# A gated sum of attention and a token mixer: w2 through the buffers of w1, and the last 64 features in both row halves

## The chip, the cores and the metric

The kernel runs on one core of a Trainium2 chip. A time is device microseconds (us) from the launch to the end on that core. The profile is one further execution, recorded instruction by instruction; its span runs from the first instruction to the last.

The engines are TensorE (PE; its weight loads are listed apart as PEld), VectorE (DVE), ScalarE (ACT), GpSimd (POOL) and SyncE (SP), which here issues all transfers.

## The reference

All is float32, with S = 2048 tokens, D = 640 channels, 32 heads of 20 channels and F = 1728 features:

```python
g = sigmoid((x * gate_w).sum(-1, keepdims=True))
a = attention(x, wq, wk, wv) @ wo           # 32 query heads share one key and one value head
h = layernorm(x)                            # (S, D)
u = gelu(einsum("sd,sf->df", h, w1) + b1)   # (D, F): the mixer works along the tokens
b = (einsum("df,fs->ds", u, w2) + b2).T     # (S, D)
out = g * a + (1 - g) * b
```

F is 13 x 128 + 64. The features are worked in 14 chunks of 128, the last of which has only 64 (`FC` = 14, `FT` = 64).

## The kernel before

**Products in three parts.** For precision each float32 operand is split into a high part, its rounding to the matmul type float32r, and a low part, the remainder. A product of two matrices is the sum of three: high by high, high by low, low by high. A block of weights is read raw from memory, and then POOL makes the high part with a copy (line 113 for w1, line 662 for w2) and the low part with a subtraction (lines 114 and 663).

**Row halves.** The 128 rows of TensorE are used as two halves of 64. A matmul with 64 rows or fewer in one half can run beside one in the other. Where both halves add into the same PSUM bank, the kernel lets only one of them do so at a time: a one-element memset on VectorE (`flag`, line 602) marks the last product of one half, and the first of the other half waits for it.

**The main loop** has 488 phases, one for each step of the attention: 32 blocks of four heads by 512 queries (`n`), each with 16 key blocks (`kb`). A phase holds

- four score matmuls for the exponentials (line 589, 62 rows), each followed by an exponential on ACT (line 592);
- four score matmuls that find the row maxima for a later block (line 419, 60 rows), each followed by a maximum on VectorE (line 422), through three PSUM banks;
- a share of the mixer's products, or of the attention's output projection, as filler (`fs`): all of it in one row half, the halves alternating from phase to phase;
- last, four matmuls of the probabilities by the values (line 616, 32 columns each, all 128 rows), which the profile shows as eight passes.

The function `beside` writes TensorE's order for a phase. One lane, in one row half, has the four scores and three of the maximum's matmuls. The other lane, in the other half, has the products, then the flag, then the tile's eviction if the tile ends here, then the fourth maximum's matmul. `beside` merges the lanes by fixed costs (0.232 and 0.147 per matmul).

**The filler.** `batches` cuts each tile's products into entries; an entry is two phases, one per row half, and gives each phase its share of that half's products. The list `seq` of entries is fixed in length, 244, and holds in this order:

- 18 tiles of w1 products (line 843: a chunk of 128 features by 320 channels, 16 token blocks, 48 products in each half), five entries each. The first ten tiles are done before the main loop;
- two empty entries, between which the first columns of w2 are read and split;
- 16 tiles of w2 products (line 682: 128 tokens by 320 channels, for both halves of the channels), four entries for each half tile. A half tile has 81 products: three for each half of the 13 full chunks, and three for the last chunk, in the lower half alone, so 42 and 39;
- eight tiles of the attention's output projection (line 791), 15 products in each half for each half tile. A half tile gets two entries as long as there are some to spare (`twice`), and then one.

What is left over goes into the last 24 steps of the attention, behind the main loop (line 748).

A half tile of products is summed in one PSUM bank, of which there is one (`ps_g`). `done` evicts it: for w2, ACT scales it and adds the bias (line 690), and a half tile later SP stores the row block to scratch memory.

**The weights.** w1 comes in blocks of 512 token rows by 128 features (`w1_load`, `w1_upto`), through three raw buffers (`w1r`) and four pairs of split ones (`w1p`), on the right side of the memory. A block is split as soon as the products of the block four before it are issued, and raw blocks are fetched two ahead. In the last chunk the 64 missing columns are set to zero (line 109). Behind the last w1 entry `second` closes these pools and opens two others: one raw buffer of seven chunks by 128 columns of w2 (`w2r`), and three pairs of split ones (`w2p`). Two of them hold the 14 chunks of one tile. `load` splits, `raw` fetches; both are hung on the entries of the tile before. The rows that the tail needs later (`spare_row`) take buffers of `w2p`.

On every engine the instructions run in the order in which the program lists them; within a phase the list is: TensorE's lanes, evictions, the postponed steps of the attention's normalisation (`settle`: a reciprocal on VectorE, line 628; a multiply on POOL, line 629; a transpose on VectorE, line 632; two splits on POOL), the loads hung on the entry (`rest`), and the values' matmuls.

Of the kernel before, what the change touches and what calls it, by code (L numbers as in the profile page):

```python
# [9 lines left out]
F32 = mybir.dt.float32  # L10
F32R = mybir.dt.float32r
# [6 lines left out]
P = 128  # L18
S, D, H, DH, F = 2048, 640, 32, 20, 1728
NS = S // P  # L20
DC = D // P
FC = (F + P - 1) // P
FT = F - (FC - 1) * P
HD2 = D // 2
# [13 lines left out]
def mix_kernel(ctx: ExitStack, tc: tile.TileContext, A_x, A_wq, A_wk, A_wv, A_wo,  # L38
               B_x, B_w1, B_b1, B_w2, B_b2, gate_w, out):
    nc = tc.nc  # L40
# [3 lines left out]
    def f32(ap):  # L44
        return ap.bitcast(F32)
# [30 lines left out]
    right = ExitStack()  # L76
    ctx.callback(right.close)
    w1r = right.enter_context(tc.tile_pool(name="w1r", bufs=3, side="right"))
    w1p = right.enter_context(tc.tile_pool(name="w1p", bufs=4, side="right"))

    HS = NS // 4
    chunks = [(d, fc, hf) for d in range(2) for fc in range(FC) for hf in range(4)]
    w1t = {}
    fetched = [0]

    w1raw = {}

    def w1_load(n):
        while len(w1raw) < min(n, len(chunks)):
            c = len(w1raw)  # L90
            d, fc, hf = chunks[c]
            fw = P if fc < FC - 1 else FT
            wr = w1r.tile([P, HS, P], F32, name="wr")
            nc.sync.dma_start(
                out=wr[:, :, :fw],
                in_=B_w1[hf * HS * P:(hf + 1) * HS * P, fc * P:fc * P + fw].rearrange("(c p) f -> p c f", p=P))
            w1raw[c] = wr

    def w1_upto(n):
        while fetched[0] < min(n, len(chunks)):  # L100
            c = fetched[0]
            w1_load(c + 1)
            d, fc, hf = chunks[c]
            fw = P if fc < FC - 1 else FT
            wr = w1raw[c]
            wh = w1p.tile([P, HS, P], F32R, name="wh")
            wl = w1p.tile([P, HS, P], F32R, name="wl")
            if fw < P:
                nc.gpsimd.memset(wr[:, :, fw:], 0.0)
            if c < 4 * PRO:  # L110
                nc.scalar.activation(wh, wr, AF.Copy)  # L111
            else:
                nc.gpsimd.tensor_copy(wh, wr)
            nc.gpsimd.tensor_sub(wl, wr, f32(wh))  # L114
            w1t[c] = wh, wl
            fetched[0] += 1
            w1_load(c + 3)
# [37 lines left out]
    with tc.tile_pool(name="pa", bufs=1) as pa, \  # L155
# [19 lines left out]
        for i in range(8):  # L175
# [11 lines left out]
        bb = pa.tile([32, P], F32, name="bb")  # L187
# [1 line left out]
        nc.sync.dma_start(out=bb[:NS, :], in_=B_b2.rearrange("(c p) -> c p", p=P))  # L189
        nc.sync.dma_start(out=bb[NS:NS + FC - 1, :],  # L190
                          in_=B_b1[:(FC - 1) * P].rearrange("(c p) -> c p", p=P))
        nc.sync.dma_start(out=bb[NS + FC - 1:NS + FC, :FT], in_=B_b1[(FC - 1) * P:][None, :])
        wkv_s = pa.tile([P, DC, P], F32R, name="wkv_s")
        nc.gpsimd.memset(f32(wkv_s), 0.0)
        mhalf = pa.tile([P, 4], F32, name="mhalf")
# [76 lines left out]
        def q_parts(m, ts):  # L272
            cols = slice(m * P, (m + 1) * P)
            return [[(wq_hi[:, c, cols], ts[c][0]) for c in range(DC)],
                    [(wq_hi[:, c, cols], ts[c][1]) for c in range(DC)],
                    [(wq_lo[:, c, cols], ts[c][0]) for c in (0, 3, 1, 4, 2)]]
# [59 lines left out]
        for sb in range(NQB):  # L336
# [14 lines left out]
            if sb == 0:  # L351
                for m in range(2):
                    p = q_parts(m, ts)
                    ahead.append(project(p[0] + p[1], more=True))
            for m in range(DC):
# [3 lines left out]
                p = q_parts(m, ts)  # L359
# [15 lines left out]
                if sb == 1 and m == 0:  # L375
                    w1_load(3)
# [131 lines left out]
    with tc.tile_pool(name="psb", bufs=2, space=PSUM, side="right") as psb, tc.manual_schedule(engines=ALL):  # L508
# [8 lines left out]
        for fc in range(PRO):  # L517
            pu = [psb.tile([P, NB], F32, name=f"pu{r}") for r in range(2)]
            for hf in range(4):
# [3 lines left out]
                wh, wl = w1t.pop(4 * fc + hf)  # L523
                for c in range(HS):
                    st = hf * HS + c
                    for k, (w, h) in enumerate(((wh, h_hi[0]), (wh, h_lo[0]), (wl, h_hi[0]))):
                        for r in range(2):
                            rows = slice(64 * r, 64 * r + 64)
                            nc.tensor.matmul(pu[r][:, :HD2], w[rows, c, :], h[rows, st, :],  # L529
                                             start=(st == 0 and k == 0), stop=(st == NS - 1 and k == 2))  # L530
                    done = [max(0, min(x, last) - skip) * (LEAD - 2) // (last - skip) for x in (at, at + 1)]
# [24 lines left out]
    pools = {}  # L556

    def second():
        right.close()
        pools["w2r"] = ctx.enter_context(tc.tile_pool(name="w2r", bufs=1, side="right"))  # L560
        pools["w2p"] = ctx.enter_context(tc.tile_pool(name="w2p", bufs=3, side="right"))

    wos = {}

# [30 lines left out]
    def other_tile(half, ins):  # L595
        if half is not None and last["half"] not in (half, None):
            tc.add_manual_dep(ins.ins, last["sig"].ins.name, SYNC, reason="row tiles that share a bank")
        last["half"], last["ins"] = half, ins
# [49 lines left out]

            later.extend((None, scale, back, high, low))

    FH = FC // 2

    def b2_jobs(st):
        hold = {}

        def load(i=0):
            wr = hold["raw"]
            wh = pools["w2p"].tile([P, FH, P], F32R, name="w2h")
            wl = pools["w2p"].tile([P, FH, P], F32R, name="w2l")
            for a, b, pr in ((0, FH - i, P),) + (((FH - 1, FH, FT),) if i else ()):  # L660
                src = wr[:pr, a:b, :]
                nc.gpsimd.tensor_copy(wh[:pr, a:b, :], src)
                nc.gpsimd.tensor_sub(wl[:pr, a:b, :], src, f32(wh[:pr, a:b, :]))
            hold["w", i] = wh, wl

        def raw(i):
            cols = slice(st * P, (st + 1) * P)
            wr = pools["w2r"].tile([P, FH, P], F32, name="w2r")
            nc.sync.dma_start(out=wr[:, :FH - i, :],
                              in_=B_w2[i * FH * P:(2 * FH - 1 if i else FH) * P, cols].rearrange("(c p) s -> p c s", p=P))  # L670
            if i:
                nc.sync.dma_start(out=wr[:FT, FH - 1, :], in_=B_w2[(FC - 1) * P:, cols])
            hold["raw"] = wr

        def mm(fc, k, d, half):
            if not hold.get("n"):
                hold["p"], hold["n"] = ps_g.tile([P, NB], F32, name="g"), 0
            wh, wl = hold["w", fc // FH]
            w, u = ((wh, u_hi), (wh, u_lo), (wl, u_hi))[k]
            hold["n"] += 1  # L680
            r = slice(64 * half, 64 * half + 64)
            other_tile(half, nc.tensor.matmul(hold["p"][:, :HD2], w[r, fc % FH, :], u[d][r, fc, :],  # L682
                             start=(hold["n"] == 1), stop=(hold["n"] == 6 * FC - 3)))

        def done(d):
            if d == 0:
                hold["t"] = fin.tile([P, D], F32, name="yo")
            t = hold["t"]
            hold["n"] = 0
            nc.scalar.activation(t[:, d * HD2:(d + 1) * HD2], hold["p"][:, :HD2], AF.Identity,  # L690
                                 bias=b2g[:, st:st + 1], scale=og_half[:, st:st + 1])
            if d == 1:
                nc.sync.dma_start(out=y_scr[st * P:(st + 1) * P, :], in_=t)

        return (lambda: raw(0)), [([[lambda h=h, fc=fc, k=k, d=d: mm(fc, k, d, h) for h in range(2 if fc < FC - 1 else 1)]
                                   for fc in range(FC) for k in range(3)],
                                  lambda d=d: done(d)) for d in range(2)], load, raw

    def load_a(st, rows, oT, yt):
        cols = slice(st * P, (st + 1) * P)  # L700
# [108 lines left out]
                       lambda d=d: done(d)) for d in range(2)]  # L809

    def spare_row(i, dt=F32):
        t = pools["w2p"].tile([P, FH, P], F32R, name=("w2h", "w2l")[i % 2])
        return t.bitcast(dt).rearrange("p a b -> p (a b)")[:, :D]

    def last_wo():
        raw = fin.tile([P, D], F32, name="yo")
# [35 lines left out]
    def batches(tiles, counts):  # L852
        out = []
        for n, (load, parts, *_) in enumerate(tiles):
            for d, (steps, done) in enumerate(parts):
                cnt = counts.pop(0)
                rows = [[f[h] for f in steps if len(f) > h] for h in range(2)]
                cut = [[len(r) * j // cnt for j in range(cnt + 1)] for r in rows]
                for j in range(cnt):
                    rest = []  # L860
                    if d == 0 and j == 0 and n + 1 < len(tiles):
                        rest.append(tiles[n + 1][0])
                    out.append(([r[c[j]:c[j + 1]] for r, c in zip(rows, cut)], rest, [done] if j == cnt - 1 else []))
        return out
# [3 lines left out]
    seq = batches([b1_jobs(*t) for t in todo], [5] * len(todo))  # L868
    for i, (steps, rest, done) in enumerate(seq):
        item, j = divmod(i + 1, 5)  # L870
        rest.insert(0, lambda c=4 * (PRO + item) + (48 * j // 5) // 12: w1_upto(c + 4))
    b2 = [b2_jobs(st) for st in range(NS)]
    seq[-1][1].extend((second, b2[0][0]))
    seq += [([[], []], [lambda: b2[0][2](0), lambda: b2[0][3](1)], []), ([[], []], [lambda: b2[0][2](1)], [])]
    m = len(seq)
    seq += batches(b2, [4] * 2 * NS)
    for st in range(NS - 1):
        seq[m + 8 * st + 2][1].append(lambda st=st: b2[st + 1][2](0))
        seq[m + 8 * st + 4][1].append(lambda st=st: b2[st + 1][3](1))
        seq[m + 8 * st + 6][1].append(lambda st=st: b2[st + 1][2](1))  # L880
    for c in range(DC):
        seq[m + 9 + 8 * c][1].append(lambda c=c: load_wo(c))
        seq[m + 11 + 8 * c][1].append(lambda c=c: split_wo(c))
# [36 lines left out]
    with tc.manual_schedule(engines={mybir.EngineType.PE, mybir.EngineType.DVE, mybir.EngineType.Activation,  # L920
# [16 lines left out]
        for k in range(k_tail):  # L937
            b = k % 2
            ss = [lambda u=u, pr=pr: qk(u, pr, b) for u in (k - 1, k) for pr in range(2) if u >= 0]
            fs, rest, done = ph[k]  # L940
# [10 lines left out]
            if k == k_tail - 4:  # L951
                raw = last_wo()
# [27 lines left out]
        for c in range(CUT // P, DC):  # L980
            r = min(P, HEAD - c * P)
# [13 lines left out]
        for i in range(4):  # L995
            st = NS - 4 + i
# [36 lines left out]
```

## Time and profile before

| | |
|---|---|
| median of three runs | 1713.4 us (1712.6 to 1716.37) |
| the profiled execution's time | 1713.95 us |
| its span | 1712.1 us |
| TensorE busy | 1699.0 us (99%) |
| VectorE busy | 1436.6 us (84%) |
| ScalarE busy | 1188.8 us (69%) |
| GpSimd busy | 565.7 us (33%) |
| mean granted TensorE clock | 0.999 |

The busy times are sums over one engine's instructions. Matmuls are pipelined and overlap, so a TensorE that is busy all the time need not be at its peak. Groups in the page's list of costliest groups are written as line, engine, operation, output<-inputs, with the shapes, then the busy time and the mean of one instruction in ns, then the idle time ahead of them and what ended it. The chain of work that ended last is followed back from the last instruction; each of its pieces is a start, a length, an engine and a line.

### The profile page before, as it was taken

To read this page: it belongs to the slowest core of one execution; us is meant where nothing else is said; L and a number is where in the kernel's file an instruction comes from. 1 tells how busy PE (TensorE), PEld (TensorE's weight loads), DVE (VectorE), ACT (ScalarE), POOL (GpSimd) and SP (SyncE) were. 2 spreads that over 40 slices of the span, in tenths; PEclk is the share of its full clock that TensorE was granted. 3 is DMA by queue.
4 is the path that set the end of the run, shared out by engine and by line. 5 is a ranking of instruction groups with operands and counts; after the bars stand their busy time and mean duration, and the time that the engine had idled before them with its cause. 6 is when DMAs were issued, how large, how long until landed. Compare 5 with 4: busy or idle time off the path is not lost.

```text
span 1712.1 us, 38812 instructions
## 1 busy us (share of the span) xinstructions
PE 1699.0 (99%) x14865; PEld 1107.1 (65%) x14865; DVE 1436.6 (84%) x2917; ACT 1188.8 (69%) x2316; POOL 565.7 (33%) x689
## 2 busy tenths in 40 slices
PE   8999999999999999999999999999999999999998
PEld 6899766666666666566666666666666666555676
DVE  5679888888888988888888888888888888888734
ACT  3444577777777777777777777777777777777675
POOL 5467545444444444232122222212211221111200
PEclk9999999999999999999999999999999999999999
DMA  6655312222222221112222222121221212344411
GB/s 188 209 165 144 99 52 60 63 72 73 58 70 64 74 62 49 50 45 69 61 68 63 63 61 58 54 55 43 55 60 55 61 54 60 86 134 118 139 57 56
DMA packets 164573, 133.86 MB, mean 78 GB/s; under 512 B 27639, under 2 KB 129428, under 8 KB 164388
## 3 DMA queue, kind: packets, MB, share of 16 engines
q1 hardware_dynamic: 164388, 131.39, 27.3%
q8 instruction: 117, 1.92, 0.5%
q14 instruction: 68, 0.56, 0.1%
HBM read 98.69 MB, written 31.65 MB: 76 GB/s over the span
## 4 chain that ended last, share of the span: by engine, by line
PE 95%; issue 2%; DVE 1%; DMA 1%; SPq 0%; ACT 0%; POOL 0%; POOLq 0%; ACTq 0%
PE o L616 30%; PE ms L419 18%; PE s L589 17%; PE g L682 11%; PE g L843 8%; PE pp L269 4%; PE pu L529 3%; PE g L791 2%; PE ms L748 1%; DVE mp L422 1%; DMA ht<-in_A_wq_dram 0%; SPq L167 0%; PE pt L261 0%; PE g L748 0%; DVE wq_lo L344 0%
## 5 line engine op out<-in xcount | busy, mean ns | idle before, releaser
L422 DVE TENSOR_REDUCE mp<-ms 128x1 f32<-128x512 f32 x2048 | 1277.6, 683 | 176.1 <-PE ms L419 174.6
L592 ACT ACTIVATE p<-s 128x512 f32<-128x512 f32 x2048 | 1069.6, 603 | 404.0 <-PE s L589 401.4
L419 PE MATMUL ms<-kst,qmx 60*128 60x512 f32 x2048 | 848.0, 422 | 3.2 <-DVE mp L422 2.4
L589 PE MATMUL s<-qst,kst 62*128 62x512 f32 x2048 | 746.6, 404 | 0.0
L616 PE MATMUL o<-p,v_sb 128*32 128x512 f32 x4096 | 554.4, 604 | 0.0
L419 PEld LDWEIGHTS ms<-kst,qmx 60*128 60x128 f32 x2048 | 378.6, 185 | 219.2 <-DVE flag L602 148.4
L589 PEld LDWEIGHTS s<-qst,kst 62*128 62x128 f32 x2048 | 378.5, 186 | 11.8 <-issue 10.9
L843 PE MATMUL g<-slot,wh 64*128 64x320 f32 x1152 | 282.5, 319 | 0.0
L843 PEld LDWEIGHTS g<-slot,wh 64*128 64x128 f32 x1152 | 191.3, 185 | 59.8 <-DVE flag L602 59.8
L682 PE MATMUL g<-slot,w2h 64*128 64x320 f32 x864 | 210.6, 319 | 0.0
L682 PE MATMUL g<-u,w2h 64*128 64x320 f32 x864 | 210.6, 319 | 0.0
L616 PEld LDWEIGHTS o<-p,v_sb 128*32 128x32 f32 x4096 | 93.2, 108 | 138.3 <-issue 131.1
L843 PE MATMUL g<-slot,wl 64*128 64x320 f32 x576 | 179.9, 312 | 0.0
L682 PEld LDWEIGHTS g<-u,w2h 64*128 64x128 f32 x864 | 142.3, 184 | 53.7 <-DVE flag L602 53.7
L682 PEld LDWEIGHTS g<-slot,w2h 64*128 64x128 f32 x864 | 142.2, 184 | 53.7 <-DVE flag L602 53.7
L629 POOL TENSOR_TENSOR ot<-ot,rl 128x512 f32<-128x512 f32 x30 | 31.6, 1052 | 405.9 <-DVE rl L628 397.2
L114 POOL TENSOR_TENSOR wl<-wr,wh 128x512 fp32r<-128x512 f32 x112 | 147.2, 1317 | 30.2 <-ACT wh L111 23.5
L682 PE MATMUL g<-u,w2l 64*128 64x320 f32 x432 | 133.4, 309 | 0.0
L682 PE MATMUL g<-slot,w2l 64*128 64x320 f32 x432 | 133.3, 308 | 0.0
L843 PEld LDWEIGHTS g<-slot,wl 64*128 64x128 f32 x576 | 106.6, 185 | 15.1 <-DVE flag L602 15.1
L791 PEld LDWEIGHTS g<-slot 64*128 64x128 f32 x480 | 70.2, 184 | 20.1 <-DVE flag L602 16.8
L791 PE MATMUL g<-slot 64*128 64x320 f32 x480 | 82.9, 316 | 0.0
(199 smaller groups left out, 1536.9 us busy)
## 6 DMA issues: line engine op xcount, KB each, us to landing
wr<-in_B_w_dram SPq DMA_DIRECT2D x104, 256.0 KB
qmx<-q_scr SPq DMA_DIRECT2D x192, 80.0 KB
qst<-q_scr SPq DMA_DIRECT2D x192, 80.0 KB
w2r<-in_B_w_dram SPq DMA_DIRECT2D x16, 448.0 KB
w2r<-in_B_w_dram SPq DMA_DIRECT2D x16, 384.0 KB
q_scr<-qh SPq DMA_DIRECT2D x20, 256.0 KB
q_scr<-ql SPq DMA_DIRECT2D x20, 256.0 KB
y_scr<-yo SPq DMA_DIRECT2D x16, 320.0 KB
```

Source lines behind the costliest of these rows:

```text
L114: nc.gpsimd.tensor_sub(wl, wr, f32(wh))
L269: nc.tensor.matmul(pp, w, t, start=first and n == 0, stop=not more and n == len(steps) - 1)
L419: nc.tensor.matmul(ms, qmax[n][64 * b:64 * b + 60, pr, qt * P:(qt + 1) * P], kst[64 * b:64 * b + 60, kq * NB:(kq + 1) * NB], start=True, s ...
L422: nc.vector.tensor_reduce(mtiles[n][:, c, kq:kq + 1], ms, axis=AX.X, op=ALU.max)
L529: nc.tensor.matmul(pu[r][:, :HD2], w[rows, c, :], h[rows, st, :], start=(st == 0 and k == 0), stop=(st == NS - 1 and k == 2))
L589: nc.tensor.matmul(s, kst[64 * b:64 * b + 62, kb * P:(kb + 1) * P], q[64 * b:64 * b + 62, pr, :], start=True, stop=True)
L592: nc.scalar.activation(p, s, AF.Exp, scale=SCALE)
L616: nc.tensor.matmul(o[32 * hh:32 * hh + 32, :], v_sb[:, kb, :], ptiles.pop((u, hh)), start=(kb == 0), stop=(kb == NS - 1), skip_group_check ...
L629: (nc.vector if spare[0] else nc.gpsimd).tensor_mul(ot, ot, rl[:, :, None].to_broadcast([P, NB // 32, 32]))
L682: other_tile(half, nc.tensor.matmul(hold["p"][:, :HD2], w[r, fc % FH, :], u[d][r, fc, :], start=(hold["n"] == 1), stop=(hold["n"] == 6 * F ...
L791: other_tile(half, nc.tensor.matmul(hold["p"][:, :HD2], o[r, c, :], w[r, c, d * HD2:(d + 1) * HD2], start=(hold["n"] == 1), stop=(hold["n" ...
L843: other_tile(half, nc.tensor.matmul(hold["p"][:, :HD2], w[r, st % HS, :], h[d][r, st, :], start=(hold["n"] == 1), stop=(hold["n"] == 6 * NS)))
```

## The change

w2's blocks are put behind w1's in the list `chunks`. They go through the same raw and split buffers, in blocks of 512 features (four chunks) by 128 tokens; the fourth block of a tile has the last two chunks. The pools are not changed between w1 and w2, and the two empty entries are gone. The next tile's blocks are split behind the sixth entry of a tile (one block), the seventh (one) and the eighth (two). The pool for the tail's rows is opened behind the last w2 entry.

The last chunk's 64 features are read twice, into the lower and the upper half of the rows (or of the columns, in w1, and of the bias). So the features' activations stand in both halves as well, and the zeroing goes. Of the three products of that chunk, two are now done in the lower half and one in the upper: 41 and 40 in place of 42 and 39.

As the list `seq` keeps its length, two entries more go to the output projection: ten half tiles of it get two entries and six get one, in place of eight and eight.

```diff
-    chunks = [(d, fc, hf) for d in range(2) for fc in range(FC) for hf in range(4)]
+    chunks = [(fc, hf) for d in range(2) for fc in range(FC) for hf in range(4)]
+    W2 = len(chunks)
+    chunks += [(st, hf) for st in range(NS) for hf in range(4)]
...
     def w1_load(n):
         while len(w1raw) < min(n, len(chunks)):
             c = len(w1raw)
-            d, fc, hf = chunks[c]
-            fw = P if fc < FC - 1 else FT
             wr = w1r.tile([P, HS, P], F32, name="wr")
-            nc.sync.dma_start(
-                out=wr[:, :, :fw],
-                in_=B_w1[hf * HS * P:(hf + 1) * HS * P, fc * P:fc * P + fw].rearrange("(c p) f -> p c f", p=P))
+            if c < W2:
+                fc, hf = chunks[c]
+                rows = slice(hf * HS * P, (hf + 1) * HS * P)
+                for o in range(0, P, P if fc < FC - 1 else FT):
+                    fw = P if fc < FC - 1 else FT
+                    nc.sync.dma_start(out=wr[:, :, o:o + fw],
+                                      in_=B_w1[rows, fc * P:fc * P + fw].rearrange("(c p) f -> p c f", p=P))
+            else:
+                st, hf = chunks[c]
+                cols = slice(st * P, (st + 1) * P)
+                nf = min(HS, FC - 1 - hf * HS)
+                nc.sync.dma_start(out=wr[:, :nf, :],
+                                  in_=B_w2[hf * HS * P:(hf * HS + nf) * P, cols].rearrange("(c p) s -> p c s", p=P))
+                if nf < HS:
+                    for o in range(0, P, FT):
+                        nc.sync.dma_start(out=wr[o:o + FT, nf, :], in_=B_w2[(FC - 1) * P:, cols])
...
     def w1_upto(n):
...
-            wr = w1raw[c]
-            wh = w1p.tile([P, HS, P], F32R, name="wh")
-            wl = w1p.tile([P, HS, P], F32R, name="wl")
-            if fw < P:
-                nc.gpsimd.memset(wr[:, :, fw:], 0.0)
+            nf = HS if c < W2 else min(HS, FC - chunks[c][1] * HS)
+            wr = w1raw[c][:, :nf, :]
+            wh = w1p.tile([P, HS, P], F32R, name="wh")[:, :nf, :]
+            wl = w1p.tile([P, HS, P], F32R, name="wl")[:, :nf, :]
...
-        nc.sync.dma_start(out=bb[NS + FC - 1:NS + FC, :FT], in_=B_b1[(FC - 1) * P:][None, :])
+        for o in range(0, P, FT):
+            nc.sync.dma_start(out=bb[NS + FC - 1:NS + FC, o:o + FT], in_=B_b1[(FC - 1) * P:][None, :])
...
     def second():
         right.close()
-        pools["w2r"] = ctx.enter_context(tc.tile_pool(name="w2r", bufs=1, side="right"))
-        pools["w2p"] = ctx.enter_context(tc.tile_pool(name="w2p", bufs=3, side="right"))
+        pools["rows"] = ctx.enter_context(tc.tile_pool(name="rows", bufs=3, side="right"))
...
         def mm(fc, k, d, half):
...
-            wh, wl = hold["w", fc // FH]
+            wh, wl = w1t[W2 + 4 * st + fc // HS]
...
+        def steps(d):
+            full = [[(fc, k), (fc, k)] for fc in range(FC - 1) for k in range(3)]
+            return [[lambda fc=fc, k=k, h=h: mm(fc, k, d, h) for h, (fc, k) in enumerate(f)]
+                    for f in full + [[(FC - 1, 0), (FC - 1, 1)], [(FC - 1, 2)]]]
...
     b2 = [b2_jobs(st) for st in range(NS)]
-    seq[-1][1].extend((second, b2[0][0]))
-    seq += [([[], []], [lambda: b2[0][2](0), lambda: b2[0][3](1)], []), ([[], []], [lambda: b2[0][2](1)], [])]
     m = len(seq)
     seq += batches(b2, [4] * 2 * NS)
     for st in range(NS - 1):
-        seq[m + 8 * st + 2][1].append(lambda st=st: b2[st + 1][2](0))
-        seq[m + 8 * st + 4][1].append(lambda st=st: b2[st + 1][3](1))
-        seq[m + 8 * st + 6][1].append(lambda st=st: b2[st + 1][2](1))
+        for j, n in ((1, 1), (2, 2), (3, 4)):
+            seq[m + 8 * st + 4 + j][1].append(lambda c=W2 + 4 * (st + 1) + n: w1_upto(c))
+    seq[-1][1].append(second)
```

More of the change, by code (lines that the diff above doesn't have):

```diff
@@ L102, in w1_upto @@
             w1_load(c + 1)
-            d, fc, hf = chunks[c]
-            fw = P if fc < FC - 1 else FT
-            wr = w1raw[c]
-            wh = w1p.tile([P, HS, P], F32R, name="wh")
-            wl = w1p.tile([P, HS, P], F32R, name="wl")
-            if fw < P:
-                nc.gpsimd.memset(wr[:, :, fw:], 0.0)
+            nf = HS if c < W2 else min(HS, FC - chunks[c][1] * HS)
+            wr = w1raw[c][:, :nf, :]
+            wh = w1p.tile([P, HS, P], F32R, name="wh")[:, :nf, :]
+            wl = w1p.tile([P, HS, P], F32R, name="wl")[:, :nf, :]
             if c < 4 * PRO:
@@ L649, in pv_mm @@
             later.extend((None, scale, back, high, low))
-    FH = FC // 2
     def b2_jobs(st):
         hold = {}
[L656 to L673, printed above, removed]
         def mm(fc, k, d, half):
@@ L681, in mm @@
             r = slice(64 * half, 64 * half + 64)
-            other_tile(half, nc.tensor.matmul(hold["p"][:, :HD2], w[r, fc % FH, :], u[d][r, fc, :],
+            other_tile(half, nc.tensor.matmul(hold["p"][:, :HD2], w[r, fc % HS, :], u[d][r, fc, :],
                              start=(hold["n"] == 1), stop=(hold["n"] == 6 * FC - 3)))
@@ L693, in done @@
                 nc.sync.dma_start(out=y_scr[st * P:(st + 1) * P, :], in_=t)
-        return (lambda: raw(0)), [([[lambda h=h, fc=fc, k=k, d=d: mm(fc, k, d, h) for h in range(2 if fc < FC - 1 else 1)]
-                                   for fc in range(FC) for k in range(3)],
-                                  lambda d=d: done(d)) for d in range(2)], load, raw
+        def steps(d):
+            full = [[(fc, k), (fc, k)] for fc in range(FC - 1) for k in range(3)]
+            return [[lambda fc=fc, k=k, h=h: mm(fc, k, d, h) for h, (fc, k) in enumerate(f)]
+                    for f in full + [[(FC - 1, 0), (FC - 1, 1)], [(FC - 1, 2)]]]
+        return (lambda: None), [(steps(d), lambda d=d: done(d)) for d in range(2)]
     def load_a(st, rows, oT, yt):
@@ L811, in spare_row @@
     def spare_row(i, dt=F32):
-        t = pools["w2p"].tile([P, FH, P], F32R, name=("w2h", "w2l")[i % 2])
-        return t.bitcast(dt).rearrange("p a b -> p (a b)")[:, :D]
+        return pools["rows"].tile([P, D], F32R, name=("row0", "row1")[i % 2]).bitcast(dt)
     def last_wo():
```

## The prediction

> **What bounds the kernel now.** I read the page's busy table and its chain of work first.
> ```profile
> PE 1699.0 (99%) x14865; PEld 1107.1 (65%) x14865; DVE 1436.6 (84%) x2917; ACT 1188.8 (69%) x2316; POOL 565.7 (33%) x689
> ...
> PE 95%; issue 2%; DVE 1%; DMA 1%; SPq 0%; ACT 0%; POOL 0%; POOLq 0%; ACTq 0%
> ```
> TensorE (PE) is busy from end to end and carries 95% of the chain that ended last; POOL has two thirds of its time free. So a change here pays by what it does to TensorE's order, and costs only if TensorE is made to wait.
>
> The main loop is a row of 488 phases, each ending in eight passes of line 616 (four matmuls, two passes each). The view of busy time by window, cut at the first pass of line 616 and asked for that line alone, therefore counts phases: x8 is one phase. Its columns are the window, its length, then TensorE's busy time and count.
> ```profile
> 711.87:724.65 12.78, 4.30 (x32) 0.67 (x32) 1.00 0.23 60
> 771.75:795.32 23.57, 8.69 (x64) 1.43 (x64) 1.00 0.31 89
> 724.65:1478.93 754.28, 278.21 (x2048) 45.73 (x2048) 1.00 0.21 58
> 1478.93:1502.32 23.39, 8.67 (x64) 1.41 (x64) 1.00 0.43 122
> 1573.50:1627.76 54.26, 17.09 (x128) 2.55 (x128) 1.00 0.50 146
> 222.28:228.12 5.84, 2.17 (x16) 0.35 (x16) 1.00 0.00 0
> 233.94:239.80 5.86, 2.17 (x16) 0.36 (x16) 1.00 0.10 22
> 239.80:245.63 5.83, 2.17 (x16) 0.35 (x16) 1.00 0.34 102
> 771.75:777.59 5.84, 2.22 (x16) 0.41 (x16) 1.00 0.48 143
> 777.59:783.56 5.97, 2.17 (x16) 0.35 (x16) 1.00 0.41 109
> 783.56:789.36 5.80, 2.13 (x16) 0.31 (x16) 1.00 0.36 106
> 789.36:795.32 5.96, 2.17 (x16) 0.35 (x16) 1.00 0.00 0
> ```
> Row by row, with the number of products per phase from the code: four empty phases between the w1 and the w2 products, 12.78 us, 3.20 each; one half tile of w2 (eight phases, 81 products), 23.57; all 32 half tiles, 754.28, or 23.57 each; eight phases of the attention output with 7 or 8 products, 23.39, or 2.92 each; sixteen with 15 products, 54.26, or 3.39 each. Then pairs of phases: three pairs of w1 with (10, 10) products, 5.84 on average; and the four pairs of a w2 half tile, which the code cuts into (9, 10), (10, 11), (10, 10), (10, 11). An empty phase costs more than one with ten products. The chain in order of time (start, length) says why:
> ```profile
> 719.42 0.48 PE ms L419 x2
> 719.90 0.69 DVE mp L422
> 720.59 0.04 issue
> 720.63 0.50 PE ms L419
> 721.13 0.46 PE s L589 x2
> 721.59 0.99 PE o L616 x8
> ```
> With no products to lie between them, the maximum's score matmuls (line 419) come in a lump, and the later of them waits 0.69 us for VectorE to free a PSUM bank.
>
> In a full phase two lanes run beside each other, one in each half of the rows:
> ```profile
> 776.28 0.30 PE L682 MATMUL g<-u,w2h 64*128 64x320 f32 x1
> 776.30 0.40 PE L419 MATMUL ms<-kst,qmx 60*128 60x512 f32 x1
> 776.43 0.30 PE L682 MATMUL g<-u,w2h 64*128 64x320 f32 x1
> 776.54 0.40 PE L589 MATMUL s<-qst,kst 62*128 62x512 f32 x1
> ```
> Products start 0.15 us apart (776.28, 776.43), score matmuls 0.24 us apart (776.30, 776.54). Seven scores take 7 x 0.24 = 1.7 us, ten products and the one score behind them 10 x 0.15 + 0.24 = 1.7 us: around ten the lanes are level. The pairs agree. From (9, 10) to (10, 10) nothing is added (5.84, and 5.84 or 5.80); from (10, 10) to (10, 11) 0.13 us (5.84 to 5.97).
>
> **The change part by part.**
>
> A, the empty phases. w2 arrives as further blocks behind those of w1, so the two empty entries of the plan (four phases) go. The number of phases stays 488, so two half tiles of the attention output get four phases with 7 and 8 products each instead of two with 15. Before: 12.78 + 4 x 54.26 / 16 = 12.78 + 13.57 = 26.35 us. After: eight phases of the kind of 1478.93 to 1502.32, 23.39 us. Gain 2.96 us. The stall in the chain above goes; what is late next in those places is TensorE itself, as in any 7-or-8 phase, and that is inside the 23.39. That window (key blocks 8 to 15 of 16) has no start of a new attention block in it, and the eight phases that take this form anew have none either: they stand at key blocks 4 to 7 and 8 to 11.
>
> B, the shared last 64 features. Both row halves now hold them, so the second of their three products moves to the other half: 42 and 39 products become 41 and 40, cut into four each. The eight phases of a half tile hold 10, 10, 10, 10, 10, 10, 10, 11 instead of 9, 10, 10, 11, 10, 10, 10, 11; 81 both times:
> ```profile
> 771.75:795.32 23.57, 14.00 (x81) 11.89 (x81) 1.00 0.31 89
> 724.65:1478.93 754.28, 448.02 (x2592) 380.62 (x2592) 1.00 0.21 58
> ```
> The last pair is unchanged (5.96), the two in the middle become (10, 10) behind a (10, 10), for which w1's pairs give 5.84. The first pair, (10, 10) behind an eleven and behind the eviction of the sum, is not in the trace. Bounds: 5.80, the w2 pair (10, 10) behind an eleven; 5.97 if the added product costs as much as the eleventh does. Nearest is the (9, 10) pair in the same place, 5.84, since a tenth product adds nothing elsewhere: I take that. Sum: 3 x 5.84 + 5.96 = 23.48, times 32 = 751.36, against 754.28: gain 2.92 us. Ends: 23.44 gives a gain of 4.20, 23.61 a loss of 1.24.
>
> C, a rule against B. The Trainium skill, page "TensorE: Matmul & The Clock Gate", section "Back-to-back issue gap", gives for isolated matmuls a gap of N / 2.4 + 2.5 ns; by an estimate from that page a product of 320 columns costs 136 ns wherever it stands, and 81 products cost the same however they are cut. The trace agrees for the eleventh product (0.13 us) and not for the tenth (0.00). By that rule B is nought, the first rival below.
>
> D, the splits on POOL.
> ```profile
> L113 POOL CAST wh<-wr 128x512 fp32r<-128x512 f32 x72 | 44.7, 621 | 91.6 <-PE g L843 84.0 <-issue 5.3 <-DMA wr<-in_B_w_dram 1.0
> L114 POOL TENSOR_TENSOR wl<-wr,wh 128x512 fp32r<-128x512 f32 x112 | 147.2, 1317 | 30.2 <-ACT wh L111 23.5 <-PE ms L419 0.9
> L662 POOL CAST w2h<-w2r 128x896 fp32r<-128x896 f32 (+2 forms) x48 | 32.7, 681 | 99.0 <-DMA w2r<-in_B_w_dram 65.7 <-PE ms L419 20.4 <-PE g L682 6.4
> L663 POOL TENSOR_TENSOR w2l<-w2r,w2h 128x896 fp32r<-128x896 f32 (+2 forms) x48 | 70.4, 1467 | 3.8
> ```
> Per 128 columns of w2, POOL now does (32.7 + 70.4) / 16 = 6.4 us; after, three blocks at 0.62 + 1.32 and a half one, some 6.8 us. Eight memsets of padding go. POOL's free time hides it. The new wait is that a block's buffers are freed by TensorE's last product out of the previous tile's block (as for w1: the 84.0 us of idle in the first row cost TensorE nothing). Block 0 is split behind the sixth of the tile's eight plan entries and needed four phases, some 11.7 us, later; the other blocks have four or more. Behind the waiting splits on POOL stands the normalising multiply, for which VectorE's transpose waits:
> ```profile
> 758.03 0.24 DVE L628 RECIPROCAL rl<-ot 128x16 f32<-128x16 f32 x1
> 758.36 1.05 POOL L629 TENSOR_TENSOR ot<-ot,rl 128x512 f32<-128x512 f32 x1 [19.52 <-DVE rl L628]
> 760.94 0.70 DVE L632 STREAM_TRANSPOSE on<-ot 128x512 f32<-128x512 f32 x1
> ```
> The multiply ends at 759.41 and the transpose starts at 760.94, 1.5 us of cover. In the new plan block 1's split stands ahead of the multiply, but is released a phase and a half earlier. I cost it at nothing; if it stood right in front of it (1.9 us), the transpose would be 0.4 us late, 6 us over 15 tiles.
>
> E, DMA. Six transfers per tile in place of three, eight more for w1's last columns, one for the bias: 48 + 8 + 1 = 57 more issues on SP.
> ```profile
> L94 SPq DMA_DIRECT2D wr<-in_B_w_dram x112: 367/374/1487, 45.1 to 673.1; - x112
> ```
> At 0.37 us that is 21 us on a queue that spans 1712. Blocks are fetched two ahead, at least two phases (5.9 us) before their split. SP may wait there some 3 us for POOL to free a raw buffer, with the next query tile queued behind it, which has twelve phases. Nothing on the path.
>
> Sum: 2.96 + 2.92 = 5.9 us off the profiled execution, 1713.95 us (span 1712.1 and 1.85 around it), gives 1708.1. The median of the runs, 1713.4, stands 0.55 below that execution: 1707.5.
>
> **The rivals.**
>
> Products cost by their number alone, not by the cut (C). For it: the eleventh's 0.13 us. Against: the tenth's nothing. A remains: 1713.4 - 2.96 = 1710.4.
>
> Slower: the first phase of a half tile waits for the eviction of the sum, there being one bank for it.
> ```profile
> 772.04 0.63 ACT L690 ACTIVATE yo<-g,b2g,og_half 128x320 f32<-128x320 f32 x1
> ...
> 772.54 0.62 ACT L592 ACTIVATE p<-s 128x512 f32<-128x512 f32 x1
> ...
> 772.79 0.41 PE L682 MATMUL g<-u,w2h 64*128 64x320 f32 x1
> ```
> It ends at 772.67, the first product starts at 772.79: 0.12 us of slack. If the shifted plan put one more exponential (0.62 us) ahead of it, each of the 32 boundaries would lose 0.50, 16 us: 1707.5 + 16 = 1723.5. It cancels the gain from 0.30 us of delay (0.12 + 5.9 / 32). Against it: the phase before a boundary has eleven products before and after, and the code puts the eviction behind the same three exponentials.
>
> Slower, less likely: block 0 comes late. It needs a delay past 11.7 - 1.9 = 9.8 us, then costs 15 times the excess; a microsecond of excess gives 1722.5.
>
> More gained: the lower end of B, and further if the leaner pairs shorten their neighbours: 1706.2 and below.
>
> **How the numbers follow.** Forecast (B between its ends; 1706.2 to 1711.7 as its own range) 0.70; B nought 0.12; eviction late 0.08; block late or POOL in the way 0.05; more gained 0.05. A measurement of this kernel can tell about 0.2%, 3.4 us, from no change. Faster than that (below 1710.0): most of the forecast and the larger gain, 0.72; within: B nought and the upper end of the forecast, 0.17; slower: 0.11. The range, 1705.0 to 1712.0, leaves out the slower cases and a large gain.
>
> **What would show it.** A: no stretch of phases without products, and only twelve phases of 15 products (3.39) in place of sixteen, the last at the same distance from the end. B: half tiles of 23.48 in place of 23.57, pairs of 5.84, 5.84, 5.84, 5.96. D: no wait of TensorE for POOL or a DMA in the w2 stretch, line 632's transposes where they were. Wrong would be a first pair near 5.97 or above, a wait of the first product for ACT, or a half tile that is uneven from tile to tile, which would point to POOL.

## The result and the profile after

The changed kernel takes 1708.95 us (median of 7 runs, 1707.89 to 1709.8), the kernel before 1713.4 us on the same chip; the ratio is 0.9975, with a 95% interval of 0.9965 to 0.9985. The change is a gain of 4.5 us. The forecast was 1707.5, a gain of 5.9.

The page's busy table and chain of the profiled execution (span 1707.7 us) hardly differ from those of before: TensorE still carries 96% of the chain.

```profile
PE 1695.3 (99%) x14865; PEld 1103.4 (65%) x14865; DVE 1437.9 (84%) x2921; ACT 1188.1 (70%) x2316; POOL 567.5 (33%) x713
...
PE 96%; issue 2%; DVE 1%; DMA 1%; SPq 0%; ACT 0%; POOL 0%; POOLq 0%; ACTq 0%
```

TensorE has the same 14865 matmuls in 3.7 us less of busy time; POOL has 24 instructions more. (Line numbers move: 616 of before is 626 here, 682 is 671, 690 is 679, 589 is 599, 592 is 602, 419 is 430, 422 is 433; the flag's 602 is 612, and 662 and 663 are 123 and 124.)

The view that counts phases is again the busy time of the last line of a phase by window: window, length, busy time and count, eight passes being one phase.

```profile
711.60:1464.48 752.88, 278.39 (x2048) 45.73 (x2048) 1.00 0.20 57
1464.48:1487.89 23.41, 8.68 (x64) 1.41 (x64) 1.00 0.39 114
1582.60:1623.31 40.71, 12.82 (x96) 1.92 (x96) 1.00 0.48 143
805.60:829.12 23.52, 8.70 (x64) 1.43 (x64) 1.00 0.44 119
805.60:811.44 5.84, 2.17 (x16) 0.35 (x16) 1.00 0.60 169
811.44:817.28 5.84, 2.18 (x16) 0.36 (x16) 1.00 0.46 121
817.28:823.13 5.85, 2.17 (x16) 0.36 (x16) 1.00 0.56 146
823.13:829.11 5.98, 2.18 (x16) 0.36 (x16) 1.00 0.16 43
```

All 32 half tiles of w2 take 752.88 us in place of 754.28; the first eight phases of the output projection 23.41, as before; the twelve phases of 15 products 40.71, or 3.39 each. The pairs of one half tile are 5.84, 5.84, 5.85 and 5.98. Put together from the starts of the phases:

| stretch | before, us | after, us | difference |
|---|---|---|---|
| up to the main loop's first value matmul | 193.2 | 193.0 | -0.2 |
| phases with w1 products | 518.7 | 518.7 | 0.0 |
| empty phases | 12.79 | none | -12.79 |
| w2, 32 half tiles | 754.28 | 752.88 | -1.40 |
| output projection, 48 and 52 phases | 148.83 | 158.83 | +10.00 |
| the last 24 steps of the attention | 70.78 | 70.78 | 0.0 |

The parts add to -4.4 us, the difference of the spans (1712.1 and 1707.7). The empty phases and the output projection together are the prediction's term A: a gain of 2.79 us, forecast 2.96. The w2 stretch is its term B: 1.40, forecast 2.92. The 0.2 us at the start is no part of the change: it differs by up to 2.6 us (191.0 to 193.6) between the runs below.

TensorE's waits in the w2 stretch, from the view of who waited for whom, are the flags between the row halves and the maxima's banks, beside 64.9 us ahead of the values' weight loads for which the view names no releaser ("issue"). POOL waits for TensorE, not the other way round. Each line has the total in us, the number of waits and the longest:

```profile
POOL wh L123 <- PE g L671: 282.1, 15, 20.1
...
PEld g L671 <- DVE flag L612: 106.5, 127, 0.8
...
PEld ms L430 <- DVE flag L612: 80.5, 96, 0.8
PEld o L626 <- issue: 64.9, 241, 0.3
...
PEld ms L430 <- DVE mp L433: 26.8, 32, 0.8
```

The 282.1 us in which POOL stood ahead of a split until TensorE was done with the buffer cost nothing.

### The profile page after: what moved, and what is told of

The parts are those of the page before. It is cut to its first block, busy times and chain, and to the rows that moved or that the text cites. A ratio compares the mean times of both kernels' runs of the same rounds, so it can differ in the third digit from the quotient of the medians.

```text
span 1707.7 us, 39022 instructions
## 1 busy us (share of the span) xinstructions
PE 1695.3 (99%) x14865; PEld 1103.4 (65%) x14865; DVE 1437.9 (84%) x2921; ACT 1188.1 (70%) x2316; POOL 567.5 (33%) x713
## 4 chain that ended last, share of the span: by engine, by line
PE 96%; issue 2%; DVE 1%; DMA 1%; SPq 0%; ACT 0%; POOL 0%; POOLq 0%; ACTq 0%
PE o L626 30%; PE s L599 18%; PE ms L430 17%; PE g L671 12%; PE g L834 8%; PE pp L280 4%; PE pu L540 3%; PE g L783 2%; PE ms L740 1%; DVE mp L433 0%; SPq L177 0%; DMA ht<-in_A_wq_dram 0%; PE pt L272 0%; PE g L740 0%; DVE wq_lo L355 0%
## 5 line engine op out<-in xcount | busy, mean ns | idle before, releaser
L834 PE MATMUL g<-slot,wh 64*128 64x320 f32 x1152 | 282.4, 319 | 0.0
L124 POOL TENSOR_TENSOR wl<-wr,wh 128x512 fp32r<-128x512 f32 (+1 forms) x176 | 220.4, 1254 | 36.3 <-ACT wh L121 22.3
L834 PEld LDWEIGHTS g<-slot,wh 64*128 64x128 f32 x1152 | 191.2, 185 | 59.9 <-DVE flag L612 59.9
L123 POOL CAST wh<-wr 128x512 fp32r<-128x512 f32 (+1 forms) x136 | 79.8, 587 | 444.9 <-PE g L671 282.1
L671 PE MATMUL g<-slot,wh 64*128 64x320 f32 x864 | 209.0, 317 | 0.0
L671 PE MATMUL g<-u,wh 64*128 64x320 f32 x864 | 208.9, 317 | 0.0
L834 PE MATMUL g<-slot,wl 64*128 64x320 f32 x576 | 179.9, 312 | 0.0
L671 PEld LDWEIGHTS g<-slot,wh 64*128 64x128 f32 x864 | 142.4, 184 | 40.2 <-DVE flag L612 39.4
L671 PEld LDWEIGHTS g<-u,wh 64*128 64x128 f32 x864 | 142.2, 184 | 40.2 <-DVE flag L612 40.2
L671 PE MATMUL g<-slot,wl 64*128 64x320 f32 x432 | 135.0, 313 | 0.0
L671 PE MATMUL g<-u,wl 64*128 64x320 f32 x432 | 134.7, 312 | 0.0
L834 PEld LDWEIGHTS g<-slot,wl 64*128 64x128 f32 x576 | 106.5, 185 | 15.1 <-DVE flag L612 15.1
L671 PEld LDWEIGHTS g<-slot,wl 64*128 64x128 f32 x432 | 79.6, 184 | 13.4 <-DVE flag L612 13.4
L671 PEld LDWEIGHTS g<-u,wl 64*128 64x128 f32 x432 | 79.4, 184 | 13.4 <-DVE flag L612 13.4
```

The costliest lines, as they stand in the source:

```text
L834: other_tile(half, nc.tensor.matmul(hold["p"][:, :HD2], w[r, st % HS, :], h[d][r, st, :], start=(hold["n"] == 1), stop=(hold["n"] == 6 * NS)))
```

## The experiments

The theory after the result: the gain is the sum of two independent parts, the phases without products that go (A) and the more even cut (B). The rival: products cost by their number alone, so that the cut is worth nothing and all that B shows is something else. Times are given as ratios to the kernel before on the same chip.

**The old cut alone undone.** In the changed kernel:

```diff
-                    for f in full + [[(FC - 1, 0), (FC - 1, 1)], [(FC - 1, 2)]]]
+                    for f in full + [[(FC - 1, k)] for k in range(3)]]
```

> The changed kernel with the old cut of the products: the last chunk's three products all in the lower half, 42 and 39. If the gain is the sum of two independent parts (the empty phases gone, 2.8 us; the more even cut, 1.4 to 1.9 us), this run keeps the first alone: 1713.4 - 2.8 = 1710.6 us, with half tiles of w2 at 23.57 us. If products cost by their number alone, the cut is worth nothing and this run is as fast as the changed kernel, 1709.0.

Measured: 1710.24 us against 1712.53 on this chip, ratio 0.9985 (0.9976 to 0.9994), a gain of 2.3 us. The interval overlaps that of the changed kernel (0.9965 to 0.9985), so the windows have to decide. Here are those of the w2 stretch and the output projection:

```profile
709.70:1464.62 754.92, 278.78 (x2048) 46.10 (x2048) 1.00 0.20 57
1464.62:1623.40 158.78, 56.41 (x416) 9.19 (x416) 1.00 0.45 131
```

The output projection is that of the changed kernel, so A stands by itself, at 12.79 + 148.83 - 158.78 = 2.84 us. The w2 stretch takes 2.04 us more than in the changed kernel, from which this run differs by the cut alone. It is 0.64 above before (754.28), which has the same cut; 0.45 of this is two pauses of ScalarE, which are dealt with below.

**The empty phases kept.** In the changed kernel:

```diff
+    seq += [([[], []], [], []), ([[], []], [], [])]
     m = len(seq)
     seq += batches(b2, [4] * 2 * NS)
```

> The changed kernel with the two empty entries put back ahead of w2's products, so that the output projection has eight and eight half tiles again. By the two parts: the even cut alone, 1713.4 - 1.6 = 1711.8 us, four empty phases of 12.8 us, half tiles of 23.51. If products cost by their number alone: 1713.4, half tiles of 23.57.

Measured: 1711.18 us against 1712.53, ratio 0.9992 (0.9983 to 1.0002): by the times alone not to be told from no change. The windows tell more:

```profile
712.06:724.84 12.78, 4.31 (x32) 0.68 (x32) 1.00 0.17 46
724.84:1476.84 752.00, 278.40 (x2048) 45.98 (x2048) 1.00 0.21 58
806.96:830.46 23.50, 8.70 (x64) 1.44 (x64) 1.00 0.29 79
```

The empty phases cost what they did, with nothing to load in them any more, so it is not the loads that made them long. The w2 stretch gains 2.28 us against before. This run has the new cut and the new buffers, so the figure alone does not part the two; the run with the old cut does, with 2.04 for the cut. The rival, by which the cut gains nothing, falls.

**The eleventh product in another place.** In the changed kernel the third product of the last chunk goes to the upper half:

```diff
-                    for f in full + [[(FC - 1, 0), (FC - 1, 1)], [(FC - 1, 2)]]]
+                    for f in full + [[(FC - 1, 0), (FC - 1, 1)]]] + [[None, lambda: mm(FC - 1, 2, d, 1)]]
```

(with a test for the None where the halves are taken apart).

> The changed kernel with the third product of the last chunk in the upper half instead of the lower (40 and 41): the eleventh product stands in the last phase but one of a half tile, and the phase with the eviction has ten. If an eleventh product costs the same wherever it stands, half tiles stay at 23.51 us and the time at 1709.0. If it costs more where the eviction of the sum stands behind it, half tiles fall by up to 0.1 us, and the time by up to 3 us, to 1706.

Measured: 1710.35 us against 1712.53, ratio 0.9987 (0.9977 to 0.9996), which overlaps the changed kernel's interval too. The w2 stretch takes 754.10 us:

```profile
711.50:1465.60 754.10, 278.94 (x2048) 46.33 (x2048) 1.00 0.20 57
```

So neither: the pair with the eleven costs 5.98 as at the end, but the first pair of the next half tile, now behind a phase of ten, takes 5.88 in place of 5.84. A pair behind an eleven is 0.04 us shorter. By the windows the place at the end is the better one, by 1.2 us.

**The eviction behind all four exponentials.** This puts the slower rival of the prediction to the test, for w2's phases alone:

```diff
-            lanes[1 - b] = lane_f(ms[1], fs, done)
+            late = 2 * m <= k < 2 * (m + 8 * NS)
+            lanes[1 - b] = lane_f(ms[1], fs, [] if late else done)
             beside(*lanes, b)
+            for f in done if late else []:
+                f()
```

> The changed kernel with w2's evictions issued behind all four exponentials of their phase instead of behind three. The prediction's slower rival priced this: 0.62 us later less 0.12 us of slack, 0.50 us at each of 32 boundaries, 16 us: 1725 us, with a first pair of phases in each half tile of 6.34 us in place of 5.84. If the eviction has more cover than the rows showed, the loss is smaller; if it is off the path altogether, 1709.

Measured: 1720.02 us against 1712.53, ratio 1.0042 (1.0026 to 1.0058), some 12 us more than the changed kernel. The chronological view of one boundary (start, length) and two windows, behind them the same boundary in the changed kernel:

```profile
805.65 0.65 ACT L679 ACTIVATE yo<-g,b2g,og_half 128x320 f32<-128x320 f32 x1
805.92 0.49 PE L430 MATMUL ms<-kst,qmx 60*128 60x512 f32 x1
806.39 0.38 PE L671 MATMUL g<-u,wh 64*128 64x320 f32 x1
```
```profile
804.86:811.09 6.23, 2.13 (x16) 0.32 (x16) 1.00 0.47 142
709.72:1474.18 764.46, 276.84 (x2048) 44.39 (x2048) 1.00 0.20 56
```
```profile
805.84 0.63 ACT L679 ACTIVATE yo<-g,b2g,og_half 128x320 f32<-128x320 f32 x1
...
806.61 0.50 PE L430 MATMUL ms<-kst,qmx 60*128 60x512 f32 x1
...
806.61 0.56 PE L671 MATMUL g<-u,wh 64*128 64x320 f32 x2
```

With the late eviction it ends at 806.30, and the first product starts at 806.39, 0.47 us behind the score matmul that it starts beside in the changed kernel. The first pair grows to 6.23, by 0.39 us, and the stretch by 764.46 - 752.88 = 11.6 us, 0.36 for each of 32. The mechanism is real, its price three quarters of the 0.50 that was forecast, and the change as it was made doesn't touch it: there the eviction ends at 806.47, 0.14 us ahead of the first product, and the first pair is 5.84.

**POOL's work on w2 tripled.** In the changed kernel:

```diff
-            nc.gpsimd.tensor_sub(wl, wr, f32(wh))
+            for _ in range(3 if c >= W2 else 1):
+                nc.gpsimd.tensor_sub(wl, wr, f32(wh))
```

> The changed kernel with the subtraction that makes the low part done three times for each block of w2 (64 blocks), some 2.6 us more of POOL's time a block, 150 us in all. If the splits are covered as the prediction has it (four phases, 11.7 us, ahead of the first use, and 1.5 us to spare at the normalising multiply), the time stays within 1 us of the changed kernel's and half tiles stay at 23.52 us. If POOL's order is close to the path, block 1's 4.5 us ahead of the multiply make VectorE's transpose late, and half tiles grow unevenly, by 0.5 us or more in every second one: 8 us or more.

Measured: 1708.82 us against 1713.71, ratio 0.9971 (0.9959 to 0.9983). The busy table and two windows:

```profile
PE 1695.3 (99%) x14865; PEld 1103.6 (65%) x14865; DVE 1436.5 (84%) x2921; ACT 1188.2 (70%) x2316; POOL 716.4 (42%) x841
```
```profile
710.10:1463.07 752.97, 278.43 (x2048) 45.77 (x2049) 1.00 0.20 58
804.11:827.62 23.51, 8.69 (x64) 1.42 (x64) 1.00 0.42 120
```

POOL does 149 us more, and w2 takes 752.97 in place of 752.88. The splits are covered with room to spare.

**Eighty and seventy-nine products.** Two runs that leave out products of the last 64 features, to price the eleventh and the tenth product of a phase. (The number of products at which a sum ends is lowered to match.)

```diff
-                    for f in full + [[(FC - 1, 0), (FC - 1, 1)], [(FC - 1, 2)]]]
+                    for f in full + [[(FC - 1, 0), (FC - 1, 1)]]]      # 80: all tens
+                    for f in full + [[(FC - 1, 0)]]]                   # 79: nine first, then tens
```

> The changed kernel without the third product of the last 64 features (low part of w2 by high part of the activations), so that each half tile has 80 products and every phase has ten. It prices the eleventh product. If it costs 0.10 to 0.14 us over the level of ten: 32 times that, 3.3 to 4.5 us less than the changed kernel, half tiles of 23.38 to 23.42 us.

> As the run with all tens, and also without the second product of the last 64 features (high part of w2 by low part of the activations): 79 products, the first phase of a half tile has nine, the others ten. If lanes are level at ten and a tenth product is free, it is as fast as the run with all tens, half tiles within 0.04 us of it. If products cost by their number alone, half tiles fall by another 0.14 us, and the time by another 4.5 us.

Measured: 1705.73 us with 80 (ratio 0.9954, 0.9939 to 0.9969) and 1706.25 with 79 (0.9953, 0.9937 to 0.9970), against 1713.71. The w2 stretch and one half tile, with 80 and then with 79:

```profile
712.23:1462.10 749.87, 279.10 (x2048) 46.45 (x2048) 1.00 0.20 57
805.78:829.20 23.42, 8.71 (x64) 1.45 (x64) 1.00 0.41 113
```
```profile
711.71:1461.48 749.77, 281.47 (x2048) 48.77 (x2048) 1.00 0.20 57
805.28:828.69 23.41, 8.80 (x64) 1.54 (x64) 1.00 0.42 113
```

From 81 to 80 products the stretch falls by 3.01 us, 0.09 for each half tile. From 80 to 79 it falls by 0.10 us in all. The eleventh product has a price; the tenth has none. (The pair that holds the eleventh is 0.14 longer, 5.98 against 5.84, and the pair behind it 0.04 shorter, which leaves 0.10 for each half tile.) That is the curve on which the even cut rests, and a price by number alone can't give it.

**The maxima dealt two and two.** Phases of 7 and 8 products cost more (2.93 us on average, away from the starts of attention blocks) than those of nine with w1 (2.90). In the changed kernel:

```diff
-... for x, c in (((b, 3), (1 - b, 1)) if len(fs) < 12 else ((b, 4), (1 - b, 0)))]
+... for x, c in (((b, 2), (1 - b, 2)) if len(fs) < 9 else ((b, 3), (1 - b, 1)) if len(fs) < 12 else ((b, 4), (1 - b, 0)))]
```

> The changed kernel with the four matmuls of the row maxima dealt two and two to the lanes in phases of fewer than nine products (the 40 phases of the output projection with 7 or 8), in place of three and one. If those phases, 2.94 us each on average, are held by the lane with seven scores, they shorten towards the 2.88 us of nine products: 40 times 0.06, 2.4 us less, 1706.6 us. If they are held by the maxima's PSUM banks, which VectorE frees, nothing is gained or the wait grows: 1709 or more.

Measured: 1707.49 us against 1713.71, ratio 0.9966 (0.9952 to 0.9979). In its trace the output projection takes 157.91 us in place of 158.83. Nearly all of that 0.9 us comes from the two places where an attention block starts. The first of these pairs falls from 6.35 (changed kernel) to 5.88 (this run):

```profile
1499.60:1505.95 6.35, 2.18 (x16) 0.36 (x16) 1.00 0.01 3
```
```profile
1498.55:1504.43 5.88, 2.27 (x16) 0.46 (x17) 1.00 0.00 1
```

In the others it is a trade: the first phase of seven gets shorter (2.98 to 2.87), the second longer (2.94 to 3.01). A second form, two and two in the phases of seven alone, ran beside the changed kernel:

> The changed kernel once more, beside the next run: a ratio to the kernel before of 0.9975, by the first measurement. If the two pauses of ScalarE in the w2 stretch (0.29 us each, in phases 397 and 423) are chance, they stand elsewhere or are gone; if the program sets them, they stand there again.

> The changed kernel with the maxima's matmuls dealt two and two in the 20 phases of seven products alone, three and one in those of eight. From the profile of the run with both: a pair of sevens 5.88 us in place of 5.92, no extra 0.45 us at the two starts of an attention block in this stretch, a pair of eights 5.80 as in the changed kernel. Gain over the changed kernel 10 x 0.04 + 0.9 = 1.3 us, over the run with both dealt two and two 0.4 us. If a phase's length depends more on its neighbours than on itself, the sum is another, and the gain may vanish.

Measured: the changed kernel 1708.06 us against 1713.43, ratio 0.9967 (0.9955 to 0.9980); the other form 1707.81, ratio 0.9968 (0.9956 to 0.9980). Of the expected 1.3 us the trace shows half: the output projection takes 158.18 us, 0.65 less than in the changed kernel. The phases of eight, dealt as in the changed kernel, did not go back to 5.80 a pair but stayed near 5.84, so a phase does depend on its neighbours. Neither form is faster than the changed kernel by anything that the times can tell.

The repeat answers the other question. The pauses of ScalarE stand in the same two phases, at the same 0.29 us; so they do in seven of the other eight runs with w2 at this place (one of these has 0.15 for the second, and the run with the late evictions has one pause, elsewhere). They are set by the program and not by chance. The first, in the chronological view of the changed kernel:

```profile
1348.18 0.60 ACT L602 ACTIVATE p<-s 128x512 f32<-128x512 f32 x1 [0.40 <-PE s L599]
1349.01 1.57 ACT L602 ACTIVATE p<-s 128x512 f32<-128x512 f32 x3 [0.23 <-PE g L671]
```
```profile
1349.65 0.14 PEld L626 LDWEIGHTS o<-p,v_sb 128*32 128x32 f32 x4 [0.20 <-ACT p L602]
```

ScalarE idles 0.23 us between two exponentials that elsewhere follow each other, and the value matmuls wait 0.20 us for it. An exponential doesn't read the products that the view names as the releaser. The kernel before has no such pause in its w2 stretch.

What holds ScalarE can be narrowed down by counting. Its list has a wait on a semaphore right ahead of that exponential, which the trace records as an instruction. From the end of this wait to the exponential 0.34 us pass, and 0.32 at the second pause; behind none of the other 270 such waits between 195 and 1630 us is it more than 0.05. With the waits counted in, the two exponentials are ScalarE's instructions 2112 and 2240 of the trace, 128 apart. In the changed kernel, its repeat and the nine variants, a wait stands directly ahead of number 1984, 2112, 2240 or 2368 in 29 places, and all 29 have this delay. The late evictions put 18 more instructions into ScalarE's list, and their one pause is at 1984; in the kernel before no wait stands ahead of such a number. So the pauses belong to steps of 128 instructions in ScalarE's list. A transfer of 8192 bytes in an instruction queue starts at 1349.65, 0.65 us after the late exponential. That makes it likely that ScalarE waits for its own instructions to be loaded, but no run tests it.

## Why the prediction came out as it did

The result, 1708.95 us, lies within the range and 1.5 us above the number; the sign and the mechanism were right. The point at which faster by 0.2% begins, 1710.0, was passed.

- **The bound.** Right: TensorE's order decides. More work on POOL changed nothing, and an eviction put behind one more exponential of 0.6 us cost 12 us.
- **A, the empty phases.** Right: 2.79 us measured, 2.96 forecast. The eight phases taken as a measure have again 23.41 us; the 32 phases of 7 and 8 products that became 40 grew by 23.56 us, 0.17 more than the forecast's 23.39.
- **B, the cut.** Right in kind, mis-sized: 1.40 us measured, 2.92 forecast. The value chosen for the unseen first pair, 5.84, was met. The shortfall of 1.52 us stands in two other places. The two pauses of ScalarE, which nothing in the trace of before announced, take 0.57; they come with the shift of ScalarE's list, not with the cut. The rest, 0.95 us or 0.03 for each half tile, is in the pairs taken as known: the last takes 5.98 in place of 5.96, the third 5.85 in place of 5.84. Such hundredths move with the program as a whole: with the empty phases kept a half tile takes 23.49 in the median, in the two forms of the last experiment, whose w2 phases are unchanged, 23.50, in the changed kernel and its repeat 23.52. Why was not found. The cut alone, between two programs that differ by nothing else, is worth 2.04 us (754.92 - 752.88), which is also less than 2.92. The step that failed is taking a gain of 0.09 us from rows rounded to 0.01 and multiplying by 32, without allowing for that.
- **C, products by their number.** It was given 0.12, and it is wrong: the tenth product is free (0.10 us over 32 half tiles), the eleventh costs 0.09 us each time. The Trainium skill's rule (page "TensorE: Matmul & The Clock Gate", section "Back-to-back issue gap") is given for isolated matmuls; here two lanes run beside each other, and up to ten products the other lane sets the end.
- **D and E, POOL and the transfers.** Right: no wait of TensorE for either, and three times the subtractions are still hidden.
- **The slower rival, the eviction.** Its mechanism is real, and it didn't occur. At full force it costs 0.36 us a boundary where 0.50 was forecast.
- **The rival of more gained.** The lower bound of the first pair, 5.80, was not reached.

## What to carry to other kernels

Where two lanes of matmuls run side by side, the price of work in one of them is a curve with a knee: count what each lane holds, find the count at which they are level, and gain by moving work from above the knee to below it. Phases without filler are not cheap (3.20 us here, 2.92 with ten products), since what remains runs into the next engine's buffers. A small gain for each of many places is best measured in a trace by the starts of a repeated instruction, and its sum should allow a hundredth of a microsecond or two per place for what the program's other parts do to it.

## What the runs showed of the hardware that was not expected

- ScalarE can pause where none of the program's waits holds it: 0.32 to 0.34 us pass from the end of a wait to its exponential, in place of 0.05, where a step of 128 instructions in ScalarE's list falls between the two. In nine of the ten runs with w2 at this place it meets the same two of the stretch's 256 phases, and it makes a phase up to 0.31 us longer.
- The time up to the main loop differs between runs from 191.0 to 193.6 us, nearly as much as the larger part of this change is worth, while the 518.7 us of the w1 phases and the 70.8 us at the end repeat within 0.2 us in every run.
